# Moving zero fills to SyncE and all loads and result stores to ScalarE in a one-token decode block (forward and backward)

## The chip, the cores and the metric

The kernel runs on one core of a Trainium2 chip. A core has five engines with instruction streams of their own: TensorE (PE in the profile), VectorE (DVE), ScalarE (ACT), GpSimd (POOL) and SyncE (SP). Data move between the device's memory (HBM) and the core's memory (SBUF) by DMA; a DMA is issued by an instruction in the stream of SyncE, ScalarE or GpSimd and is carried by 16 DMA engines. The metric is device time of one execution in microseconds, the median of the runs.

## The reference

One token passes through an attention block with a sliding window over a key/value cache and then a gated bilinear block; the kernel returns the output and the gradients with respect to every input but `B_x`.

```python
D = 448; Hq, Hkv, Sk, Dh = 16, 8, 32768, 256; F = 1792; W = 4096
h  = x + attention(layernorm(x), k_cache[:, :, -W:], v_cache[:, :, -W:], wq, wo)
xn = layernorm(h)
h2 = h + ((xn @ w_gate) * (xn @ w_up)) @ w_down
out, vjp = jax.vjp(f, x, k_cache, v_cache, wq, wo, w_gate, w_up, w_down)
return (out, *vjp(grad_out))
```

All tensors are bf16. The caches have 32768 positions in each of 8 groups and only the last 4096 are used, so the gradients of both caches (`out_2` for K, `out_3` for V, 134 MB each) are zero in 28672 of 32768 rows. Those zeros must be written: 8 groups x 2 tensors x 7 blocks of 2 MB, 235 MB in all. The remaining traffic is about 104 MB: K and V of the window (16 loads of 2 MB), four V loads again for the backward part, the weights (wq twice), 16 stores of 2 MB for the nonzero parts of `out_2` and `out_3`, and the gradients of the weights.

## The kernel before, in words

The kernel is written against a tile framework: it names tiles and operations, and the framework decides the order of instructions in each engine's stream and puts in the semaphores. Each engine executes its stream in order; a DMA instruction that must wait on a semaphore holds everything behind it in that stream. Nearly all of SBUF is one tile, `arena`, cut up by hand with `ar(offset, n)`.

Two names choose the issuing engines (L37, L38): `LD` issues the loads and the stores of results, `ZQ` the zero fills.

1. *Start (L87 to L213).* `zeros`, a region of 8192 columns in each of 128 partitions, is cleared half by VectorE (L87) and half by GpSimd (L88). `LD` loads x, grad_out and wq (L90 to L96). The loop at L114 to L120 issues 103 zero fills of 2 MB on `ZQ`, all reading from `zeros`. `load_kv` (L187) and L194 load K and V of the first groups and `w_down` (`wd_sb`). `layernorm` (L152) uses ScalarE for the square root (L157) and VectorE for its reciprocal (L158) and the rest; L206 and L210 compute q. At L218 VectorE makes 14 products of `w_down` with grad_out, each with a sum, into `d_hh`; they are used only in the middle stage.
2. *Attention (L258 to L324), over 8 groups.* `scores(g + 1)` is called before `moments(g)`. `dots` (L235) transposes K by TensorE (L243), ScalarE copies the transposed blocks back (L260), and row products (L246) make the scores; VectorE copies them (L248) and a softmax follows (L262 to L287). `moments` scales K by the probabilities on VectorE (L298) and multiplies by V on TensorE (L302, L306); ScalarE copies the result (L309). K has three slots and V four (`HELD`); the next load into a slot (L319, L321) waits until TensorE and VectorE have read it.
3. *Middle (L326 to L458).* `wo`, `w_gate` and `w_up` are loaded at L323 to L328 and the layernorm, gated block and its backward are computed, with long runs of VectorE products (L387, L412). `out_0` is stored at L444, and L453 to L458 form the gradient of q.
4. *Backward over 8 groups (L528 to L608).* Each group's V is transposed and multiplied (`dots`), then 16 pairs of TensorE products (L574) fill PSUM tiles `d_ps`, which VectorE (L581, L582) and ScalarE (L578, L579) copy in turn to two of three buffers `stage`. Two stores of 2 MB (L584) send them out. The buffers go round: a later group can't overwrite one until its store has landed. Between groups, the jobs in `plan` (L523) form weight gradients on VectorE (L467, L497) in two buffers `wst` and store them at L478 (`out_5`), L483 (`out_8`), L490 and L505 (`out_6`, `out_7`), L510 and L520 (`out_4`).
5. *Late fills (L610 to L613).* Five fills, 4 of 4 MB and 1 of 2 MB, read `zeros` and the V slot behind it, which L589 clears in the seventh group. They are issued on `LD`, in among the last stores.

The framework guards each DMA with one of a set of completion semaphores that it gives out in turn; a DMA can be issued only when the previous DMA on its semaphore has landed. In the kernel before, GpSimd's fills have one set of eight and SyncE's DMAs another set of eight.

Of the kernel before, what the change touches and what calls it, by code (L numbers as in the profile page):

```python
# [25 lines left out]
ZW = 8192  # L26
# [6 lines left out]
def kernel(  # L33
        ctx, tc, A_x, A_k_cache, A_v_cache, A_wq, A_wo, B_x, B_w_gate, B_w_up, B_w_down, grad_out,
           out_0, out_1, out_2, out_3, out_4, out_5, out_6, out_7, out_8):
    nc = tc.nc
    LD = nc.sync  # L37
    ZQ = nc.gpsimd  # L38

    const = ctx.enter_context(tc.tile_pool(name="const", bufs=1))  # L40
    small = ctx.enter_context(tc.tile_pool(name="small", bufs=2))
# [5 lines left out]
    VB = 16 * KB  # L47
# [5 lines left out]
    def ar(off, n):  # L53
        return arena[:, off:off + n]
# [34 lines left out]
    x_bf = const.tile([1, D], bf16)  # L89
    LD.dma_start(out=x_bf[:], in_=A_x.rearrange("a b d -> (a b) d"))  # L90
    dh2_bc = const.tile([128, D], bf16)
    LD.dma_start(out=dh2_bc[:], in_=grad_out.rearrange("a b d -> (a b) d").to_broadcast([128, D]))
    wq_A = A_wq[0:384, :].rearrange("(p c) j -> p c j", c=3)
    wq_B = A_wq[384:D, :].rearrange("r (h j) -> (r h) j", h=2)
    LD.dma_start(out=wqA, in_=wq_A)
    LD.dma_start(out=wqB, in_=wq_B)  # L96

# [11 lines left out]
    def zero_rows(o, g, n0, n1, f):  # L109
        reg = o[0, g, 0:Sk - W, :].rearrange("s d -> (s d)")[n0 * 128 * ZW:n1 * 128 * ZW]  # L110
        return reg.rearrange("(n p f) -> n p f", p=128, f=f)

    late_jobs = [(out_2, G - 1, 5, 7, 2 * ZW), (out_3, G - 1, 0, 6, 2 * ZW), (out_3, G - 1, 6, 7, ZW)]
    for g in range(G):  # L114
        for o in (out_2, out_3):
            if g == G - 1 and o is out_3:
                continue
            reg = zero_rows(o, g, 0, 5 if g == G - 1 else NZ, ZW)
            for i in range(reg.shape[0]):
                ZQ.dma_start(out=reg[i], in_=zeros)  # L120

# [65 lines left out]
    def load_kv(dst, cache, g):  # L187
        LD.dma_start(out=dst, in_=cache[0, g, Sk - W:, :].rearrange("(p t) d -> p t d", t=T))

# [3 lines left out]
    load_kv(V_slot[1], A_v_cache, 1)  # L193
    LD.dma_start(out=wd_sb, in_=B_w_down.rearrange("(h p b) n -> p h b n", h=2, b=NB))  # L194
    load_kv(K_slot[2], A_k_cache, 2)
# [250 lines left out]
    with tc.tile_pool(name="work2", bufs=2) as work2, tc.tile_pool(name="lnw", bufs=1) as lnw, \  # L446
# [163 lines left out]
        for o, g, n0, n1, f in late_jobs:  # L610
            reg = zero_rows(o, g, n0, n1, f)
            for i in range(reg.shape[0]):
                LD.dma_start(out=reg[i], in_=ar(VB + ZW - f, f))  # L613

# [1 line left out]
_INS = ['A_x', 'A_k_cache', 'A_v_cache', 'A_wq', 'A_wo', 'B_x', 'B_w_gate', 'B_w_up', 'B_w_down', 'grad_out']  # L616
# [26 lines left out]
```

## Time and profile before

| what | value |
|---|---|
| median of three runs | 817.24 us (814.16, 817.24, 819.33) |
| profiled execution's span | 819.2 us |
| busy: TensorE, VectorE, ScalarE, GpSimd | 452.5, 366.3, 192.6, 60.0 us |
| DMA moved | 339.01 MB, mean 414 GB/s over the span |
| GpSimd's queue (q0): packets, MB, share of 16 DMA engines | 14832, 216.01, 62.3% |
| SyncE's queue (q1) | 9494, 122.48, 35.4% |
| GpSimd's 103 fills: issue to landing, median | 59.9 us |
| SyncE's 2 MB stores, issue to landing, median | 27.5 us |
| HBM read, written | 57.89 MB, 280.59 MB |

The profile is one execution. Its span runs from the first to the last instruction. Idle time of an engine is put down to what ended it. "SPq", "DVEq" and the like name the part of an engine that issues and waits; a DMA's landing is the moment when its completion semaphore is full. In the page's slices each digit is the busy share of a fortieth of the span in tenths, 9 meaning 90% or more.

### The profile page before, as it was taken

The page shows a single profiled execution, that of the slowest core. Times are in us where ns is not written, and L with a number is a line of the kernel's source. Part 1 is how long each engine was busy: PE and PEld are TensorE (multiplying, and loading weights), DVE is VectorE, ACT ScalarE, POOL GpSimd, SP SyncE. Part 2 cuts the span into 40 slices and gives each one's busy share as a digit, 9 for nine tenths or more (in the row PEclk, how much of TensorE's full clock was granted, in tenths as well). Part 3 has the DMA queues.
Part 4 walks back from the last instruction along what each step waited for, and adds up shares of the span by engine and source line. Part 5 has one row for each costly group of instructions (what it writes and reads, how often), then busy time and mean ns, then how long its engine had stood idle before and what let it go on. Part 6 is the DMA issues. An engine that isn't in the chain of part 4 may idle for free.

```text
span 819.2 us, 8365 instructions
## 1 busy us (share of the span) xinstructions
PE 452.5 (55%) x3151; PEld 242.9 (30%) x3151; DVE 366.3 (45%) x1153; ACT 192.6 (24%) x301; POOL 60.0 (7%) x112
## 2 busy tenths in 40 slices
PE   0566999999999997510937817352430437111000
PEld 0332545545545554210833413220210213000000
DVE  3023762562652652489234927354455447334000
ACT  0232134134043110200112606141230235123000
POOL 4000000000001100111110000000000000000000
PEclk9967999999999997565876967755655577555555
DMA  8999999999999999999999999999999999999991
GB/s 332 429 427 434 430 426 431 429 429 426 431 428 426 431 413 423 430 429 430 420 425 422 412 428 419 414 426 417 429 413 428 430 430 427 427 424 436 422 413 59
DMA packets 24366, 339.01 MB, mean 414 GB/s; under 512 B 2691, under 2 KB 3334, under 8 KB 4358
## 3 DMA queue, kind: packets, MB, share of 16 engines
q0 software_dynamic: 14832, 216.01, 62.3%
q1 hardware_dynamic: 9494, 122.48, 35.4%
q8 instruction: 24, 0.39, 0.2%
q14 instruction: 16, 0.13, 0.0%
HBM read 57.89 MB, written 280.59 MB: 413 GB/s over the span
## 4 chain that ended last, share of the span: by engine, by line
DMA 28%; DVE 10%; PE 8%; ACT 2%; issue 1%; another core or an unknown queue 1%; SPq 0%; DVEq 0%; ACTq 0%
DMA out_dram<-arena 28%; DVE arena L412 2%; PE rows_ps L246 2%; PE d_ps L574 2%; DVE arena L581 2%; DVE arena L582 2%; PE tr_ps L243 1%; PE dqb_ps L453 1%; DVE arena L467 1%; ACT arena L579 1%; ACT arena L534 1%; DVE arena L387 0%; DVE arena L566 0%; DVE arena L536 0%
## 5 line engine op out<-in xcount | busy, mean ns | idle before, releaser
L298 DVE TENSOR_SCALAR arena<-arena,p_f 128x256 bf16<-128x256 bf16 x512 | 109.3, 280 | 63.0 <-PE M_ps L302 63.0
L574 PE MATMUL d_ps<-arena,rT 32*128 32x512 bf16 x256 | 41.5, 520 | 163.5 <-ACT arena L579 117.3
L302 PE MATMUL M_ps<-arena 128*128 128x512 bf16 x512 | 124.3, 384 | 0.0
L243 PE MATMUL tr_ps<-ident_bf,arena 128*128 128x128 bf16 x1024 | 88.2, 237 | 34.7 <-DVE arena L536 14.4
L120 POOL DMA_DIRECT2D out_dram<-arena x103 | 55.4, 539 | 665.0 <-DMA out_dram<-arena 665.0
L246 PE MATMUL rows_ps<-arena,vpad 128*16 128x512 bf16 x256 | 86.7, 438 | 24.8 <-DVE arena L536 16.4
L243 PEld LDWEIGHTS <-arena 128*128 128x128 bf16 x1024 | 66.3, 106 | 71.3 <-issue 58.9
L260 ACT COPY arena<-tr_ps 128x1024 bf16<-128x1024 bf16 x64 | 61.7, 1015 | 99.0 <-PE tr_ps L243 99.0
L582 DVE CAST arena<-d_ps 128x512 bf16<-128x512 f32 x64 | 43.6, 681 | 84.7 <-DMA out_dram<-arena 84.7
L574 PEld LDWEIGHTS <-rT 32*128 32x128 bf16 x256 | 10.5, 96 | 186.1 <-issue 145.9
L579 ACT CAST arena<-d_ps 128x512 bf16<-128x512 f32 x64 | 38.0, 594 | 108.6 <-DMA out_dram<-arena 108.6
L302 PEld LDWEIGHTS <-arena 128*128 128x128 bf16 x512 | 46.4, 99 | 51.3 <-issue 7.4
L306 PE MATMUL ok_ps<-arena 128*16 128x256 bf16 x512 | 58.7, 274 | 0.9 <-DVE arena L287 0.9
L578 ACT CAST arena<-d_ps 128x512 bf16<-128x512 f32 x64 | 37.6, 588 | 69.9 <-PE d_ps L574 69.8
L581 DVE CAST arena<-d_ps 128x512 bf16<-128x512 f32 x64 | 43.9, 686 | 21.4 <-PE d_ps L574 21.0
L306 PEld LDWEIGHTS <-arena 128*16 128x16 bf16 x512 | 45.2, 90 | 15.6 <-issue 5.1
L534 ACT COPY arena<-tr_ps 128x1024 bf16<-128x1024 bf16 x32 | 32.5, 1015 | 54.3 <-PE tr_ps L243 49.7
L246 PEld LDWEIGHTS <-vpad 128*16 128x16 bf16 x256 | 19.6, 91 | 72.8 <-issue 63.9
L309 ACT COPY arena<-M_ps 128x512 f32<-128x512 f32 x16 | 8.6, 589 | 80.0 <-PE M_ps L302 80.0
L536 DVE COPY arena<-tr_ps 128x1024 bf16<-128x1024 bf16 x32 | 21.8, 683 | 3.6 <-PE tr_ps L243 3.6
L467 DVE TENSOR_SCALAR arena<-arena,xT 128x1792 bf16<-128x1792 bf16 (+1 forms) x9 | 8.0, 893 | 33.1 <-DMA out_dram<-arena 21.5
L412 DVE CUSTOM_DVE_ANT_0 arena<-arena,dh_bc 128x448 bf16<-128x448 bf16 x32 | 20.0, 624 | 1.1
(184 smaller groups left out, 339.0 us busy)
## 6 DMA issues: line engine op xcount, KB each, us to landing
out_dram<-arena POOLq DMA_DIRECT2D x103, 2048.0 KB, 59.9
out_dram<-arena SPq DMA_DIRECT2D x17, 2048.0 KB, 27.5
arena<-in_A_v_cache_dram SPq DMA_DIRECT2D x12, 2048.0 KB, 39.2
arena<-in_A_k_cache_dram SPq DMA_DIRECT2D x8, 2048.0 KB, 21.3
out_dram<-arena SPq DMA_DIRECT2D x4, 4096.0 KB, 42.5
arena<-in_A_wq_dram SPq DMA_DIRECT2D x2, 3072.0 KB
arena<-in_A_wo_dram SPq DMA_DIRECT2D x1, 3584.0 KB
out_dram<-arena SPq DMA_DIRECT2D x3, 1024.0 KB, 44.1
```

Source lines behind the costliest of these rows:

```text
L120: ZQ.dma_start(out=reg[i], in_=zeros)
L243: nc.tensor.transpose(tr_ps[:, dh, i, :], X_sb[:, 4 * q + i, dh * 128:(dh + 1) * 128], ident_bf[:])
L246: nc.tensor.matmul(rows_ps[:], lhsT=pad[:, dh, 16 * q:16 * q + 16], rhs=XT[:, dh].rearrange("p t k -> p (t k)"), start=(q == 0 and dh == 0 ...
L260: sT_ps = dots(K_slot[g % 3], KT_slot, vpad[g % 2], rows1, ps_c, "cols", lambda q, XT, ps: nc.scalar.copy(out=XT, in_=ps))
L298: nc.vector.tensor_scalar(out=pK[:, i, hh, :], in0=K_sb[:, t, :], scalar1=p_f[:, 8 * i + c, hh:hh + 1], scalar2=None, op0=ALU.mult)
L302: nc.tensor.matmul(M_ps[:, vh, :], lhsT=V_sb[:, t, vh * 128:(vh + 1) * 128], rhs=pK[:, i, :, :].rearrange("p h d -> p (h d)"), start=(t == ...
L306: nc.tensor.matmul(ok_ps[:, k, :], lhsT=ppad[g % 2][:, 8 * (t % 4) + t // 4, :], rhs=X_sb[:, t, :], start=(g == 0 and k == 0 and t == 0), ...
L534: nc.scalar.copy(out=XT, in_=ps)
L574: nc.tensor.matmul(d_ps[:, qi].rearrange("p w d -> p (w d)"), lhsT=rT[32 * q:32 * (q + 1), :], rhs=RB_[32 * q:32 * (q + 1), l, :], start=T ...
L579: nc.scalar.copy(out=stK[:, t:t + 2, :], in_=d_ps[:, :, 1, :])
L581: nc.vector.tensor_copy(out=stV[:, t:t + 2, :], in_=d_ps[:, :, 0, :])
L582: nc.vector.tensor_copy(out=stK[:, t:t + 2, :], in_=d_ps[:, :, 1, :])
```

## The change

SyncE issues all zero fills, the 103 early ones and the five late ones, and nothing else. ScalarE issues all loads and all stores of results, 63 DMAs, in the one stream with its copies and activations. GpSimd issues no DMA. No transfer, size, buffer or computation is changed. What the framework then makes of it: SyncE's 108 and ScalarE's 63 DMAs share one set of eight completion semaphores, given out in one common order; and the order of instructions on the other engines shifts, among other places at the start, where VectorE's 14 products at L218 now stand ahead of the reciprocal at L158.

```diff
@@ -34,8 +34,8 @@
     nc = tc.nc
-    LD = nc.sync
-    ZQ = nc.gpsimd
+    LD = nc.scalar
+    ZQ = nc.sync
 
@@ -610,7 +610,7 @@
         for o, g, n0, n1, f in late_jobs:
             reg = zero_rows(o, g, n0, n1, f)
             for i in range(reg.shape[0]):
-                LD.dma_start(out=reg[i], in_=ar(VB + ZW - f, f))
+                ZQ.dma_start(out=reg[i], in_=ar(VB + ZW - f, f))
```

## The prediction

> **What bounds the kernel now.** I read the page's slices and queues first, then stretches of the span by window, then the waits of GpSimd and SyncE, then the timelines at the places that the change touches.
>
> ```profile
> DMA  8999999999999999999999999999999999999991
> GB/s 332 429 427 434 430 426 431 429 429 426 431 428 426 431 413 423 430 429 430 420 425 422 412 428 419 414 426 417 429 413 428 430 430 427 427 424 436 422 413 59
> q0 software_dynamic: 14832, 216.01, 62.3%
> q1 hardware_dynamic: 9494, 122.48, 35.4%
> ```
>
> The DMA engines are full in every slice but the first and the last, at about 427 GB/s. GpSimd's zero fills (q0) are 216 MB, all the rest (q1) 122.5 MB. Nothing runs faster while 339 MB must pass; the engines are off the bound. What matters is whether the DMA engines ever run dry.
>
> ```profile
> 420.00:790.00 370.00, 133.12 (x932) 61.19 (x931) 167.96 (x345) 102.19 (x166) 18.66 (x35) 0.62 1.01 424
> 789.00:814.20 25.20, 0.00 (x0) 0.00 (x0) 0.00 (x0) 0.00 (x0) 0.00 (x0) 0.50 0.45 192
> ...
> POOL out_dram L120 <- DMA out_dram<-arena: 665.0, 95, 12.4
> SPq L638 <- DMA out_dram<-arena: 51.0, 1, 51.0
> ```
>
> The first two lines are stretches (length, busy of five engines, clock, DMA share, GB/s). From 420 to 790 us the rate is 424 GB/s. In the last 25 us the share is 0.45: some of the 16 engines end much before others, which wastes 25.2 x 0.55 = 13.9 us. GpSimd waits 665 us at L120: it always has eight fills under way and issues the next when one lands, so fills are never missing. SyncE's last wait ends near 814 us; some 5 us of span follow.
>
> ```profile
> 75.26 0.63 DVE L218 CUSTOM_DVE_ANT_0 arena<-arena,dh_bc 128x448 bf16<-128x448 bf16 x1 [9.02 <-DMA arena<-in_B_w_down_dram]
> ...
> 22.39 0.19 PE L206 MATMUL qT_ps<-X_b,arena 128*128 128x2 bf16 x1 [12.29 <-DMA arena<-in_A_wq_dram]
> 32.25 1.89 PE L243 MATMUL tr_ps<-ident_bf,arena 128*128 128x128 bf16 x16 [6.71 <-DMA arena<-in_A_k_cache_dram]
> 51.68 0.93 PE L243 MATMUL tr_ps<-ident_bf,arena 128*128 128x128 bf16 x7 [5.43 <-DMA arena<-in_A_k_cache_dram]
> 99.30 0.90 PE L243 MATMUL tr_ps<-ident_bf,arena 128*128 128x128 bf16 x13
> ...
> 45.10 0.68 DVE L248 COPY arena<-rows_ps 16x512 f32<-16x512 f32 x1 [18.95 <-PE rows_ps L246]
> 57.47 3.22 DVE L298 TENSOR_SCALAR arena<-arena,p_f 128x256 bf16<-128x256 bf16 x16
> ...
> 402.74 0.34 SPq L490 DMA_DIRECT2D out_dram<-arena  x1
> ```
>
> These (start, length) date the start: q from 22.4 us, scores of group 0 from 32.3, w_down at 75.3, group 0's moments done at 99.3. ScalarE's copies at L260 then repeat every 31.3 us (100.01, 131.34, 162.66), TensorE being 99% busy. The first large result is stored at 402.7.
>
> **The change, part by part.**
>
> *Issue cost.* An issue on SyncE's queue lasts 0.34 to 0.74 us (L490 above is 0.34). ScalarE takes over 63 of them, 63 x 0.5 = about 32 us in all; it is busy 24% and the DMA engines hide it. GpSimd loses 103 issues of 0.54 us, which held nobody up. The sum has 0 for both. Uncovered, an issue between copies at L578/L579 costs 0.5 us, at most 32.
>
> *Fills tied to the rest.* This is the main term. Before, GpSimd's fills had eight completion semaphores of their own. In the changed program's order all 171 DMAs of SyncE and ScalarE take turns on one set of eight, and each waits until the previous user of its semaphore has landed. At most eight are in flight, and a fill can stand behind a load or store that ScalarE has not been able to issue. The first place where this bites: the 64th fill waits for the store of out_6 at L490 to land. Ahead of it stand 63 fills and all loads, 178 MB. At the rates above the DMA engines are through with them at about 420 us (1 us either way). If L490 issues by then nothing is lost; each us later is lost whole.
>
> *When L490 issues.* The order also moves VectorE's 14 products with w_down (L218) ahead of the first layernorm's reciprocal (L158). The bytes ahead of w_down in its own queue are the same, and the opposite queue is full of fills as before, so it lands again at about 75.3 us; but now everything waits for it. The chain: 75.3 + 14 x 0.67 for L218 (0.67 is the spacing of such products at L412) = 84.7; + 1.4 from reciprocal to X_b (as in the second layernorm, 321.22 to 322.66); + 3.1 for q (22.39 to 25.5); + 0.5; + 10.7 for group 0's scores (32.25 to 45.10, less 2.1 for two transposed blocks that now go ahead of q); + 6.1 softmax (45.10 to 57.47, less 6.3 spent on K of group 1); + 26 for the moments of group 0 with the scores of group 1 (57.47 to 99.30 is 41.8, less 9.0 of waiting for w_down and less 9.4 of its products, is 23.4; TensorE's own work gives 26, which I take). Sum 132.5 against 99.3: 33 us late. ScalarE's own waits are no part of it: its twelfth load, the last before the square root (L157), waits for the fifth fill, which at half rate (9.8 us a fill) lands near 54. In the attention its loads wait for fills that landed earlier, so the period stays 31.3. From 99.3 to 402.7 nothing is shortened that I count on, except 1 us: L490 issues at 435 (418 if only half of the delay survives, 443 if the loads in the middle stage come later).
>
> *After L490.* 339 - 178 = 161 MB are left, at 424 GB/s 380 us: 435 + 380 = 815. Around it the fills are released only as out_6, out_7 and out_5 (L505, L490, L478) land, and a landing takes some 2 us beyond its bytes (x_bf: issued at 0.74, used at 3.23). Two or three such gaps: + 5. Then the stages of the last eight groups: each group's copies wait for the previous group's store (19.9 us at 724.9 in the chain) and then need about 14 us. Between the pairs of stores at L584 the new order puts four to seven fills; with the pair and the jobs that is 29 to 59 us of transfer, more than the 12 + 14 us that a store and the copies behind it need. So transfer stays the bound there, and ScalarE waiting for a semaphore holds up only copies that are early: 0, at most + 15.
>
> *The end.* The late fills (L613) no longer stand behind the stores: SyncE has five transfers, 18.9 MB, to go with the last stores, so there is no bare tail. Of the 13.9 us of uneven ends I keep 3, because the dry spell at 420 us lets all 16 engines start level again (bounds 0 and 14). In the trace's packet records a 16 KB packet takes 618.7 ns in GpSimd's queue and 612.3 in SyncE's; for the 6,300 packets of fills left after L490 that is 6,300 x 6.4 / 16 = 2.5 us less (bounds 0 and 3).
>
> *The sum:* 435 + 380 + 5 + 3 - 2.5 + 5 (after the last landing) = 825 us, against the profiled execution's 819.2. That execution is 0.24% above the median of the three runs, 817.24, so the forecast for a median is 823.
>
> *A rule of the skill.* Before the change, V of group 1 and w_down (3.70 MB) took 51.68 to 75.26, 157 GB/s, where V of group 0 and K of group 1 (4.19 MB) took 32.25 to 51.68, 216 GB/s: w_down's small packets get less than half. The Trainium skill, page "DMA: Bandwidth & Descriptors", section "Queues, rings and completion order", says that each engine serves its queues in turn, packet by packet, and gives SP and ACT a row each. The trace agrees for GpSimd against SyncE; no run here yet shows SyncE against ScalarE.
>
> **The rivals.**
>
> *Nothing changes.* The fills and the rest are the same transfers on the same engines, and both ends of every wait exist before. 819 less the packets' 2.5, so 815 for a median. For it: DMA is full in 38 slices. Against it: one set of semaphores instead of two. The same skill page, section "Issuing engines are not separate DMA queues", holds that the issuing engine matters only for issue time; by that rule this is the case.
>
> *No dry spell, and even engines (faster).* If group 0 is less than 17 us late, L490 issues by 420 and the fills never run out. Then 339 MB at 427 is 794, plus 5 for the slow first slice and 5 at the end: 804, + 2 for a landing gap, 806. It is decided by whether VectorE's wait for w_down is shorter than 75 us. For it: SyncE's packets are quicker and uneven ends may be GpSimd's queue alone. Against it: VectorE's order and the landing at 75.26. The skill's page, section "Latency and other measured facts", suspects GpSimd's descriptor rings of slowing two engines.
>
> *Uneven engines stay and ScalarE's waits hit the copies.* 825 + 11 (all 14 kept) + 15 in the eight groups = 851; half of it 838.
>
> *One line for both queues.* If fills and loads were served strictly in the order of issue, a store would wait behind up to seven fills, 34 us, not 12; 34 + 14 is 48 against 29 to 47 us of transfer: some 15 us in each of five groups, 825 + 75 = 900. Against it: nothing in this trace pairs SyncE with ScalarE.
>
> **How the numbers follow.** Forecast 0.40 (its own range 813 to 834), nothing changes 0.15, faster 0.16, uneven and waiting 0.22, one line 0.07. About 1% (809 to 825) is what a measurement of this kernel can tell. Faster: the third case and a little of the first, 0.18; same: the second and half of the first, 0.37; slower: the rest, 0.45. The range 805 to 850 leaves out the last case and the ends.
>
> **What would show it.** Right: VectorE's L218 before L158 with a wait until 75 us; moments of group 0 done near 132; a slice or two near 420 to 440 us with DMA well under 9; L490 near 435; no long waits of SyncE at L120 elsewhere; a last slice that ends sharply. Wrong: DMA at 9 throughout (no dry spell), group 0 before 116, or DMA slices of 7 and 8 all through the last eight groups.

## The result and the profile after

The changed kernel takes 823.99 us (median of 17 runs, 821.78 to 827.09) against 817.24 us (17 runs, 813.97 to 825.69): ratio 1.0061, 95% interval 1.0035 to 1.0086. It is slower by 0.6%, under the 1% that was named as measurable in advance but outside zero. Ratios here use the runs that were not in a slow state and need not equal the quotient of two medians. The profiled execution after is 824.0 us, before 819.2 us: 4.8 us to explain.

The page of the changed kernel, slices and queues (q1 is SyncE, q10 ScalarE; GpSimd's q0 is gone):

```profile
DMA  8999999999999999999945999999999999999997
GB/s 329 432 430 434 428 428 429 429 428 430 429 429 425 429 427 427 413 428 429 431 190 236 405 414 428 434 425 401 424 433 426 429 426 432 430 430 431 433 436 328
q1 hardware_dynamic: 15552, 234.89, 67.1%
q10 hardware_dynamic: 8774, 103.60, 30.0%
```

Two things differ from before: a dry spell in slices 21 and 22 (4 and 5 tenths), and a last slice of 7 where there was a 1. Stretches of the changed kernel (length, busy of the five engines, clock, DMA share, GB/s):

```profile
420.00:430.00 10.00, 3.41 (x10) 1.93 (x11) 7.13 (x31) 0.00 (x0) 0.00 (x0) 0.50 0.12 52
430.00:440.00 10.00, 10.00 (x50) 8.88 (x49) 2.30 (x4) 1.19 (x2) 0.00 (x0) 0.79 0.01 2
440.00:450.00 10.00, 9.58 (x61) 8.07 (x60) 6.13 (x11) 2.71 (x5) 0.00 (x0) 1.00 0.83 347
460.00:790.00 330.00, 164.36 (x912) 68.74 (x911) 166.36 (x332) 100.79 (x166) 0.00 (x0) 0.59 1.01 425
818.00:824.00 6.00, 0.00 (x0) 0.00 (x0) 0.00 (x0) 0.00 (x0) 0.00 (x0) 0.50 0.25 107
```

From 420 to 450 the missing share is 8.8 + 9.9 + 1.7 = 20.4 us. From 460 to 790 nothing is missing. The kernel before ended otherwise; its stretch from the point where the share falls to its last landing:

```profile
795.00:814.00 19.00, 0.00 (x0) 0.00 (x0) 0.00 (x0) 0.00 (x0) 0.00 (x0) 0.50 0.29 122
```

That is 19 x 0.71 = 13.5 us missing, and 5 us with no transfer follow. So 20 us are lost in the middle and some 14 us come back at the end. Two timelines of the changed kernel, VectorE's and ScalarE's, show why the dry spell ends when it does:

```profile
75.80 0.63 DVE L218 CUSTOM_DVE_ANT_0 arena<-arena,dh_bc 128x448 bf16<-128x448 bf16 x1 [67.34 <-DMA arena<-in_B_w_down_dram]
...
85.02 0.15 DVE L158 RECIPROCAL mv<-mv 1x1 f32<-1x1 f32 x1
101.10 0.68 DVE L248 COPY arena<-rows_ps 16x512 f32<-16x512 f32 x1 [10.60 <-PE rows_ps L246]
```

```profile
56.17 1.28 ACT L157 ACT_TABLE_LOAD   x1 [56.17 <-DMA out_dram<-arena]
...
129.05 1.07 ACT L309 COPY arena<-M_ps 128x512 f32<-128x512 f32 x2 [9.13 <-PE M_ps L302]
...
136.02 0.34 ACTq L188 DMA_DIRECT2D arena<-in_A_k_cache_dram  x1
...
439.77 0.37 ACTq L490 DMA_DIRECT2D out_dram<-arena  x1
```

VectorE waits 67 us for w_down, and the first reciprocal comes after its products. Group 0's moments are copied out at 129.05 (before: 97.45), L490 issues at 439.8 (before: 402.7), and the DMA engines run again from 440. SyncE's waits at L120 confirm who is waiting (us in total, times, longest), and its timeline shows the 64th fill:

```profile
SPq L120 <- DMA out_dram<-arena: 402.1, 51, 35.6
...
444.45 0.81 SPq L120 DMA_DIRECT2D out_dram<-arena  x2
```

The longest, 35.6 us, is the one for out_6: the 63rd fill is issued at 408.5 and the 64th, which has out_6's semaphore, at 444.45, when out_6 has landed. SyncE also waits up to 30.5 us at L120 for a V load and 29.7 us for `wo`, where the prediction expected no other long wait; the DMA engines stay full in those waits. The median fill takes 31.3 us from issue to landing, against 59.9 before: fills wait in SyncE, not in the DMA engines.

### The profile page after: what moved, and what is told of

Its sections match the earlier page's. It is cut to its first block, busy times and chain, and to the rows that moved or that the text cites. A ratio compares the mean times of both kernels' runs of the same rounds, so it can differ in the third digit from the quotient of the medians.

```text
span 824.0 us, 8353 instructions
## 1 busy us (share of the span) xinstructions
PE 481.8 (58%) x3151; PEld 250.4 (30%) x3151; DVE 374.2 (45%) x1153; ACT 190.6 (23%) x301; POOL 4.6 (1%) x9
## 5 line engine op out<-in xcount | busy, mean ns | idle before, releaser
L298 DVE TENSOR_SCALAR arena<-arena,p_f 128x256 bf16<-128x256 bf16 x512 | 110.0, 283 | 59.5 <-PE M_ps L302 59.5
L574 PE MATMUL d_ps<-arena,rT 32*128 32x512 bf16 x256 | 58.1, 545 | 120.0 <-DVE arena L582 82.5
L243 PE MATMUL tr_ps<-ident_bf,arena 128*128 128x128 bf16 x1024 | 99.5, 251 | 41.0 <-DMA arena<-in_A_k_cache_dram 25.0
L302 PE MATMUL M_ps<-arena 128*128 128x512 bf16 x512 | 121.5, 380 | 0.0
L243 PEld LDWEIGHTS <-arena 128*128 128x128 bf16 x1024 | 73.1, 112 | 96.8 <-issue 70.5
L246 PE MATMUL rows_ps<-arena,vpad 128*16 128x512 bf16 x256 | 96.2, 470 | 7.6 <-DVE arena L536 3.0
L260 ACT COPY arena<-tr_ps 128x1024 bf16<-128x1024 bf16 x64 | 61.6, 1014 | 135.9 <-PE tr_ps L243 135.9
L302 PEld LDWEIGHTS <-arena 128*128 128x128 bf16 x512 | 46.0, 98 | 51.9 <-issue 6.3
L574 PEld LDWEIGHTS <-rT 32*128 32x128 bf16 x256 | 12.6, 97 | 157.0 <-issue 91.2
L581 DVE CAST arena<-d_ps 128x512 bf16<-128x512 f32 x64 | 44.1, 688 | 34.8 <-PE d_ps L574 34.7
L306 PE MATMUL ok_ps<-arena 128*16 128x256 bf16 x512 | 58.2, 273 | 0.9 <-DVE arena L287 0.9
L306 PEld LDWEIGHTS <-arena 128*16 128x16 bf16 x512 | 45.1, 90 | 13.8 <-issue 3.4
L218 DVE CUSTOM_DVE_ANT_0 arena<-arena,dh_bc 128x448 bf16<-128x448 bf16 x14 | 8.7, 624 | 67.8 <-DMA arena<-in_B_w_down_dram 67.3
L536 DVE COPY arena<-tr_ps 128x1024 bf16<-128x1024 bf16 x32 | 22.0, 687 | 13.5 <-PE tr_ps L243 12.5
L458 ACT ACTIVATE arena<-dqb_ps 128x512 bf16<-128x512 f32 x8 | 4.8, 597 | 68.1 <-PE dqb_ps L456 59.7
L412 DVE CUSTOM_DVE_ANT_0 arena<-arena,dh_bc 128x448 bf16<-128x448 bf16 x32 | 20.0, 624 | 1.1
## 6 DMA issues: line engine op xcount, KB each, us to landing
out_dram<-arena SPq DMA_DIRECT2D x104, 2048.0 KB, 31.3
out_dram<-arena ACTq DMA_DIRECT2D x16, 2048.0 KB, 21.8
out_dram<-arena ACTq DMA_DIRECT2D x3, 1024.0 KB, 13.3
```

What stands on the lines that cost most here:

```text
L243: nc.tensor.transpose(tr_ps[:, dh, i, :], X_sb[:, 4 * q + i, dh * 128:(dh + 1) * 128], ident_bf[:])
L246: nc.tensor.matmul(rows_ps[:], lhsT=pad[:, dh, 16 * q:16 * q + 16], rhs=XT[:, dh].rearrange("p t k -> p (t k)"), start=(q == 0 and dh == 0 ...
L260: sT_ps = dots(K_slot[g % 3], KT_slot, vpad[g % 2], rows1, ps_c, "cols", lambda q, XT, ps: nc.scalar.copy(out=XT, in_=ps))
L298: nc.vector.tensor_scalar(out=pK[:, i, hh, :], in0=K_sb[:, t, :], scalar1=p_f[:, 8 * i + c, hh:hh + 1], scalar2=None, op0=ALU.mult)
L302: nc.tensor.matmul(M_ps[:, vh, :], lhsT=V_sb[:, t, vh * 128:(vh + 1) * 128], rhs=pK[:, i, :, :].rearrange("p h d -> p (h d)"), start=(t == ...
L306: nc.tensor.matmul(ok_ps[:, k, :], lhsT=ppad[g % 2][:, 8 * (t % 4) + t // 4, :], rhs=X_sb[:, t, :], start=(g == 0 and k == 0 and t == 0), ...
```

## The experiments

Questions: is it the late attention, through the shared semaphores, that costs the time? And why are the ends even now? The rivals: ScalarE's issuing, the queue that carries the fills, or the dry spell as a thing that levels the engines.

**e1: the first layernorm ahead of the loads** (the changed kernel otherwise).

```
+    rstd1, xnT_f, X1_b = layernorm(x_bf[:], bf16, "ln1")
     load_kv(K_slot[0], A_k_cache, 0)
     ...
-    rstd1, xnT_f, X1_b = layernorm(x_bf[:], bf16, "ln1")
```

> The changed kernel with the first layernorm written ahead of the loads of K, V and w_down, so that its square root on ScalarE and its reciprocal on VectorE no longer stand behind the wait for w_down; the fills stay tied to the loads and stores. Theory (the dry spell at 420 to 440 us costs the time, because L490 comes late, and the even ends belong to the fills being on SyncE's queue): group 0 is done near 120 us instead of 136, L490 issues at 420 to 426 instead of 440, the dry spell shrinks from 20 us to 0 to 6, and the time is 805 to 812. Rival 1 (the even ends are only a gift of the dry spell): L490 moves as above but the last 25 us are uneven again, some 10 us come back, time 815 to 820. Rival 2 (the dry spell is not what sets the time): 822 to 826, as the changed kernel.

Measured: 812.64 us, ratio to the kernel before 0.9913 (0.9878 to 0.9948). The moments of group 0 are copied at 114.5, L490 issues at 425.6. Its stretches:

```profile
420.00:430.00 10.00, 9.58 (x58) 8.06 (x58) 3.64 (x6) 3.29 (x5) 0.00 (x0) 1.00 0.45 188
430.00:440.00 10.00, 10.00 (x66) 9.23 (x66) 6.00 (x14) 1.79 (x3) 0.00 (x0) 1.00 0.75 310
...
790.00:805.00 15.00, 0.00 (x0) 0.00 (x0) 0.00 (x0) 0.00 (x0) 0.00 (x0) 0.50 0.99 424
805.00:811.20 6.20, 0.00 (x0) 0.00 (x0) 0.00 (x0) 0.00 (x0) 0.00 (x0) 0.50 0.16 69
```

The dry spell falls from 20 to 8 us, the ends stay even, and the span falls by 12.8 us. The dry spell and the time end just above the theory's 0 to 6 us and 805 to 812. One moved line turns the split into a gain of 0.9%: the loss against the kernel before came from the order that the change brought about. The tie still costs the 8 us that are left.

**e5: the products with w_down done twice.**

```
-    for h in range(2):
+    for h in [0, 1] * 2:
```

> The changed kernel with the 14 products with w_down done twice (the second time gives the same numbers), all ahead of the first layernorm's reciprocal on VectorE. It adds 14 x 0.67 = 9.4 us of VectorE work at about 85 us and no transfer. Theory (each us by which L490 is late past 420 us is lost whole): group 0 near 145, L490 near 449, dry spell 29 us, time 833 (829 to 836). Rival (the delay is taken up by slack, since DMA is the bound and VectorE is idle most of the span): 822 to 826.

Measured: 834.83 us, ratio 1.018 (1.0134 to 1.0225); the span is 833.4, 9.4 more than the changed kernel's. L490 is at 448.6, 8.8 later.

```profile
420.00:430.00 10.00, 0.00 (x0) 0.00 (x0) 9.48 (x31) 0.00 (x0) 0.00 (x0) 0.50 0.69 293
430.00:440.00 10.00, 4.56 (x13) 2.83 (x14) 6.05 (x27) 0.00 (x0) 0.00 (x0) 0.50 0.00 0
440.00:450.00 10.00, 10.00 (x54) 9.04 (x54) 2.30 (x4) 1.79 (x3) 0.00 (x0) 0.85 0.09 35
```

VectorE is idle for more than half of the span, and yet 9.4 us of work on it near 85 us cost 9.4 us at the end. Of these, 8.8 are in the dry spell (29.3 us missing against 20.5); the other 0.6 is less than two executions of one kernel differ by.

**e6: the same in the kernel before.**

> The kernel before with the 14 products with w_down done twice: the control of e5. It delays VectorE by 9.4 us near 85 us, but the fills have semaphores of their own and nothing waits for L490. Theory: L490 near 412, no dry spell, time within 2 us of the kernel before (815 to 820). Rival (lateness of the attention costs in any split): 824 to 829, with the loss at the end of the run.

Measured: 819.61 us, ratio 0.9994 (0.9953 to 1.0035). No cost, as expected, but it proves less than was meant: here the products stand between the multiplications of the moments and fill waits there, and L490 issued at 403.7, not 412. The delay never reached the stores, so this says nothing on lateness without the tie; e3 does.

**e3: late attention without the tie** (fills on GpSimd, all else on ScalarE).

```
     LD = nc.scalar
-    ZQ = nc.sync
+    ZQ = nc.gpsimd
     ...
-                ZQ.dma_start(out=reg[i], in_=ar(VB + ZW - f, f))
+                LD.dma_start(out=reg[i], in_=ar(VB + ZW - f, f))
```

> Fills on GpSimd as in the kernel before, loads and stores on ScalarE as in the changed one, late fills (L613) on ScalarE too. GpSimd's fills have semaphores of their own; VectorE's order is the changed kernel's. Theory (tie makes the dry spell; GpSimd's queue makes the uneven ends): no dry spell at 420 to 440 us, L490 after 430, uneven ends of 10 to 14 us as before, and up to 15 us more because the last stage starts 33 us later and ScalarE issues the late fills between its copies: 815 to 830. Rival (moving loads and stores to ScalarE costs time by itself, its waits holding up copies): above 830, with DMA slices of 7 or 8 in the last third. Rival (the unevenness was the pairing of GpSimd with SyncE): 804 to 812.

Measured: 823.32 us, ratio 1.0031 (1.0004 to 1.0058). L490 is as late as in the changed kernel, 437.8, and there is no dry spell at 420 to 440. But:

```profile
420.00:440.00 20.00, 15.33 (x70) 12.56 (x71) 7.61 (x29) 1.79 (x3) 2.54 (x5) 0.70 1.00 424
754.00:764.00 10.00, 1.22 (x6) 0.31 (x6) 2.46 (x4) 1.11 (x3) 0.00 (x0) 0.50 0.24 102
...
800.00:808.00 8.00, 4.76 (x18) 0.92 (x16) 5.16 (x8) 5.21 (x10) 0.00 (x0) 0.50 0.00 0
```

The fills were not held back at 420, and from 754 nothing is left of GpSimd's queue; the last pair of stores (L584, at 809.3; before 758.9) finds the DMA engines idle ahead of it. So time is lost without the tie too, as the upper part of the theory's range had it, but at the end of the run. That the late attention alone costs it is not shown. From L490 to the last pair of stores the kernel before takes 356 us and e3 372, and e3's late fills (L613) stand among ScalarE's copies:

```profile
760.09 0.58 ACT L579 CAST arena<-d_ps 128x512 bf16<-128x512 f32 x1 [18.27 <-DMA out_dram<-arena]
...
763.49 0.34 ACTq L613 DMA_DIRECT2D out_dram<-arena  x1
```

ScalarE waits 18 us for a store to land, and the next late fill is issued only behind that wait, while the DMA engines have a share of 0.24. So the rival has a part in it: its slices of 7 and 8 are there (7, 8, 8 and 4 at the end of the page's DMA row), though the time stays below its 830. How much is lateness and how much ScalarE's order of issue, no run separates.

**e4: fills on SyncE, loads and stores on GpSimd.**

```
-    LD = nc.scalar
+    LD = nc.gpsimd
     ZQ = nc.sync
```

> The fills on SyncE as in the changed kernel, but loads and stores on GpSimd, so that the fills have completion semaphores of their own and wait only for other fills. VectorE's order keeps the products with w_down ahead of the reciprocal, so group 0 and L490 stay late. Theory (the tie through the eight shared semaphores makes the dry spell, not the late attention by itself): no slice under 8 between 400 and 460 us although L490 issues after 430. Time then by the ends: with even ends (unevenness belongs to the queue that carries the fills, GpSimd's) 804 to 812; with uneven ends (unevenness comes with any run without a dry spell, or with any use of GpSimd's queue) 814 to 822. Rival (the late attention itself leaves nothing to transfer near 420 us): the dry spell stays and the time is 820 to 826.

Measured: 816.21 us, ratio 0.9968 (0.9938 to 0.9999). It misses as a test of lateness: with ScalarE free of loads the square root and the reciprocal (14.7 us) come early again and L490 is at 413.7. It is of use for the ends. Fills on SyncE's queue end unevenly too:

```profile
795.00:811.00 16.00, 0.00 (x0) 0.00 (x0) 0.00 (x0) 0.00 (x0) 0.00 (x0) 0.50 0.46 196
```

**e7 and e8: the products moved off the path.** In both, the 14 products move from L216 into the loop over the groups and wait for the softmax of group 2; e7 is e1 with this, e8 the kernel before with this.

```
+            if g == 1:
+                nc.vector.tensor_scalar(out=one_late[:], in0=p_next[:, 0, 0:1], scalar1=0.0, scalar2=1.0, op0=ALU.mult, op1=ALU.add)
+                nc.vector.tensor_scalar(out=dh2_bc[:], in0=dh2_bc[:], scalar1=one_late[:], scalar2=None, op0=ALU.mult)
+                for h in range(2):
+                    for b in range(NB):
...
```

> The changed kernel with the first layernorm ahead of the loads, as in e1, and the 14 products with w_down made to wait for the softmax of group 2 (their second operand is multiplied by a 1.0 that is worked out from it), so that no engine waits for w_down near 75 us. DMAs, queues, semaphores and their order are those of e1. Theory (dry spell = how late L490 is past 420): group 0 done at 82 to 92, L490 at 387 to 400, no slice under 9 between 400 and 460. Then the ends decide what the uneven ends of the kernel before came from. If from GpSimd's queue: the last 20 us are as sharp as in the changed kernel, time 802 to 808. If every run without a dry spell ends unevenly: 812 to 818. Rival (the tie costs by itself, in the last eight groups): DMA slices of 7 or 8 after 500 us and 815 or more.

> The kernel before (fills on GpSimd, loads and stores on SyncE), with the products made to wait for the softmax of group 2 as in e7: the control of e7 for the attention's earlier end alone. Theory (the kernel before is bound by transfers; its fills are never missing, its ends are uneven): L490 near 387 to 395, the rest as before, 815 to 820. Rival (it is the earlier attention, not the split, that gains in e7): 803 to 810.

Measured: e7 811.61 us, ratio 0.991 (0.9878 to 0.9942); e8 818.54 us, ratio 0.9978 (0.9939 to 1.0016). In e8 L490 issues at 396.4, 6 us earlier than in the kernel before, so the earlier attention alone gains nothing that can be told, as the theory had it. e7 fell short: group 0 is done at 102, not 82 to 92, because ScalarE now stands at its twelfth load (timeline of ScalarE in e7, where the copies of L260 are L257):

```profile
62.55 0.34 ACTq L188 DMA_DIRECT2D arena<-in_A_v_cache_dram  x1
62.93 1.93 ACT L257 COPY arena<-tr_ps 128x1024 bf16<-128x1024 bf16 x2 [58.26 <-DMA arena<-in_A_v_cache_dram]
```

L490 issues at 416.2, ahead of 420, and still some time is lost:

```profile
422.00:429.00 7.00, 6.99 (x44) 6.28 (x43) 0.77 (x3) 0.60 (x1) 0.00 (x0) 1.00 0.42 178
...
804.00:809.00 5.00, 0.00 (x0) 0.00 (x0) 0.00 (x0) 0.00 (x0) 0.00 (x0) 0.50 0.17 72
```

The next fill needs out_6 to have landed, not to have been issued. In the trace's records of out_6's semaphore the first of 16 increments comes at 422.6 and the last at 428.13, 12 us after the issue; the next fill is issued at 428.15. So 416 was too late by some 6 us or more, for the share falls from 422 on.

**e9, e10, e11: earlier still.** e9 is e7 with the loads of K and V of group 2, V of group 3 and w_down moved behind the scores of group 0 and so between ScalarE's copies. e10 and e11 also move the loop of the fills behind the loads and hold it back until K of group 0, or V of group 1, has landed.

```
         p_next = scores(0)
+        load_kv(K_slot[2], A_k_cache, 2)
+        load_kv(V_slot[2], A_v_cache, 2)
+        load_kv(V_slot[3], A_v_cache, 3)
+        LD.dma_start(out=wd_sb, in_=B_w_down.rearrange("(h p b) n -> p h b n", h=2, b=NB))
```

```
+    nc.gpsimd.tensor_scalar(out=zeros[:, 0:1], in0=K_slot[0][:, 0, 0:1], scalar1=0.0, scalar2=None, op0=ALU.mult)
+    for g in range(G):
+        for o in (out_2, out_3):
...
```

> e7 with the loads of K and V of group 2, V of group 3 and w_down written after the scores of group 0, so that ScalarE issues them between its copies and not ahead of them. In e7 its first copy waited until 62.9 us behind the twelfth load. Runs so far say: span = 804 + the time for which the DMA engines ran dry near 420 to 440 us (after 20, e1 8, e7 4, e5 29). Theory: copies of group 0 start near 32 us and end near 58, group 0 done at 84 to 92, L490 at 395 to 408, no dry spell at all. If the uneven ends of the kernel before belong to the use of GpSimd's queue: last 20 us sharp, span 803 to 806, median 804 to 809. If it takes a dry spell, however short, to make the 16 engines end together: a tail of 8 to 14 us of low share returns, 812 to 818.

> e9 with the zero fills made to wait until K of group 0 has landed (GpSimd writes one column of the zero tile from K times 0.0), so that the first loads have the DMA engines to themselves. All DMAs stay on SyncE and ScalarE. By the program, 61 fills then stand ahead of the first that waits for a large store (L505, the store after L490), about 174 MB, which are through near 412 us. Theory: K lands near 18 us and not 32, group 0 done at 70 to 82, L490 at 380 to 398, the fills never run out, no slice under 8 from the second to the last but one. If even ends belong to having nothing on GpSimd's queue: last 20 us sharp, span 803 to 806, median 804 to 808. If they come from a dry spell: a tail of 8 to 14 us of low share, span 812 to 818. Rival (a dry spell comes anyway, by another wait): dry spell of x us, span 804 + x.

> e10 with the fills waiting for V of group 1 instead of K of group 0, that is some 15 us later; 58 fills stand ahead of the first that waits for L505, about 168 MB, through near 398 us. Theory: L490 at 372 to 390, again no dry spell and the same two cases for the ends: span 803 to 806, or 812 to 818. It tells whether more lead of the attention is worth anything once no transfer is missing (theory: nothing, within 2 us of e10). If the loads alone do not keep the DMA engines full in the first 40 us, the second slice shows it and the span is longer by that.

Measured: 812.49 us (ratio 0.9898, 0.986 to 0.9937), 811.35 us (0.9922, 0.9895 to 0.9949), 810.87 us (0.9917, 0.9884 to 0.995). L490 came to 414.1, 400.3 and 386.1 (expected: 395 to 408, 380 to 398, 372 to 390), but each reordering also changed which fill stands behind which store, and the fills ran out earlier as well: 7.7, 5.0 and 4.3 us were missing between 340 and 460. No version was without a dry spell, which none of the three expected, so these runs could not settle what makes the ends even. They end within 2 us of e1 and e7; e11, with the lowest median, is 0.8% below the kernel before.

**e12 and e13: a dry spell made on purpose, in kernels without the tie.** e12 is the kernel before, e13 is e4, each with one wait: all fills under way have to land after the 53rd.

```
                 ZQ.dma_start(out=reg[i], in_=zeros)
+                if (o, g, i) == (out_3, 3, 3):
+                    nc.gpsimd.memset(zeros[:, 0:1], 0.0)
```

> The kernel before, with one wait added: after its 53rd fill GpSimd writes a zero into the zero tile, for which all fills under way (at most eight) have to land first, so that the DMA engines run dry once near 385 us, at a time when SyncE has nothing to transfer. Fills stay on GpSimd, nothing is tied to L490. Theory (the 16 engines drift apart as long as no DMA waits for all of them, whatever queue carries the fills; a dry spell lets them start level): a dry tail of some 7 us near 385, and at the end a tail of 4 us in place of the 19 us of the kernel before; span 804 + 6 + 2 + 3 = 815, so 0.3 to 0.8% less than the kernel before in spite of the wait. Rival (uneven ends belong to GpSimd's queue and come at the end in any case): the tail stays over 12 us and the wait is paid on top, span 824 to 828, 0.5 to 1% more.

> e4 (fills on SyncE, loads and stores on GpSimd, two sets of semaphores) with the wait of e12: after the 53rd fill all fills under way have to land once, near 380 us. It tells apart why the last stretch after a dry spell ended with a tail of 12 us in e12 and of 3 to 5 us in the changed kernel, e1, e5, e7, e9, e10 and e11. Theory A (it is the queue that carries the fills): fills are on SyncE here, so the tail after the wait is 3 to 5 us, span 804 + 6 + 2 + 3 = 815. Theory B (it is the shared set of eight semaphores, by which fills, loads and stores wait for each other): the two sets are apart here, so the tail is 10 to 13 us as in e12, span 818 to 824. Both expect a tail of 6 to 8 us at the wait near 380.

Measured: e12 823.13 us, ratio 1.0041 (1.0006 to 1.0076); e13 819.22 us, ratio 1.0008 (0.9975 to 1.004). Stretches at the wait and at the end, e12 first, then e13:

```profile
371.00:380.00 9.00, 0.00 (x0) 0.00 (x0) 8.51 (x29) 0.00 (x0) 0.41 (x2) 0.50 0.18 78
...
806.00:818.00 12.00, 0.00 (x0) 0.00 (x0) 0.00 (x0) 0.00 (x0) 0.00 (x0) 0.50 0.39 168
```

```profile
371.00:383.00 12.00, 2.09 (x9) 1.81 (x9) 9.19 (x31) 0.00 (x0) 0.10 (x1) 0.50 0.30 128
...
809.00:816.00 7.00, 0.00 (x0) 0.00 (x0) 0.00 (x0) 0.00 (x0) 0.00 (x0) 0.50 0.13 56
```

At 371 both queues show the same tail: the 16 engines are 8 to 10 us apart after 370 us, whichever queue carries the fills. After the dry spell GpSimd's fills end with a tail of 12 us, SyncE's with one of 7. The theory that a dry spell is enough falls: e12 was to be faster than before and is slower, as its rival had it (span 824 to 828; it is 824.6). e13 lies between its two theories: its tail of 7 us is nearer to theory A, the queue of the fills, its span of 817.3 nearer to theory B.

The traces hold a more direct measure. They record 16 increments of a DMA's semaphore, as many as there are DMA engines. I take the time from the first increment to the last as the lag between the first and the last engine. For the fills that land in each stretch and have all their increments on record it is (us; the first two kernels, without a dry spell, are divided at 425 us):

| kernel | fills on | from 340 us to the dry spell | from there to 480 us | largest, 700 to 760 us |
|---|---|---|---|---|
| before | GpSimd | 8.6 to 12.8 | no dry spell; 11.0 to 17.5 | 44.1 |
| e4 | SyncE | 9.3 to 14.2 | no dry spell; 13.6 to 19.4 | 25.9 |
| e12 | GpSimd | 7.5 to 8.0 | 0.4 to 4.0 | 29.8 |
| e13 | SyncE | 9.3 to 13.7 | 0.2 to 3.2 | 14.8 |
| after | SyncE | 7.4 to 13.8 | 0.2 to 1.5 | 8.9 |
| e11 | SyncE | 9.1 to 9.8 | 1.7 to 6.5 | 15.0 |

In all of them the lag is 1 to 5 us around 100 us and grows, also where nothing is issued on GpSimd (after, e11). The dry spell takes it down, to 0.2 to 0.4 us in the first fills of e12, e13 and the changed kernel. So a dry spell does level the engines, on either queue. What differs is how fast they drift apart again: in these profiles faster with fills on GpSimd (e12) than on SyncE. e13 is no worse than e11, which has the shared set.

**All spans by one sum.** For each profile I added length x (1 - DMA share) over stretches of 10 us, a share above 1 counting as 1, with one last stretch from 780 us to the end (e6 is left out: its profiled execution, 829.32 us, lies 10 us above its median):

| kernel | span us | missing 340 to 460 | missing from 780 | missing elsewhere | span less all missing |
|---|---|---|---|---|---|
| before | 819.2 | 0.0 | 18.4 | 4.3 | 796.5 |
| after | 824.0 | 20.5 | 4.8 | 3.7 | 795.0 |
| e1 | 811.2 | 8.6 | 5.6 | 3.7 | 793.3 |
| e5 | 833.4 | 29.3 | 5.9 | 3.4 | 794.8 |
| e3 | 821.7 | 0.1 | 13.3 | 11.4 | 796.9 |
| e4 | 812.6 | 0.0 | 10.4 | 6.1 | 796.1 |
| e7 | 809.0 | 4.1 | 4.1 | 3.7 | 797.1 |
| e8 | 816.5 | 0.0 | 16.8 | 3.2 | 796.5 |
| e9 | 810.6 | 7.7 | 5.2 | 4.1 | 793.6 |
| e10 | 809.5 | 5.0 | 7.1 | 3.0 | 794.4 |
| e11 | 809.3 | 4.3 | 7.0 | 3.7 | 794.3 |
| e12 | 824.6 | 8.0 | 13.8 | 4.9 | 797.9 |
| e13 | 817.3 | 8.4 | 7.5 | 5.8 | 795.6 |

The last column stays within 5 us while the spans differ by 24: the time of every version is its transfers plus the time in which DMA engines had nothing to do.

## Why the prediction came out right, point by point

*The bound.* Right. The table above is the statement that nothing runs faster while 339 MB must pass.

*The tie and the dry spell (the main term).* Right in mechanism and size: the fills ran out at 420, as worked out, and came back with L490. That each us past 420 is lost whole is shown by e5 (L490 8.8 us later, 8.8 us more missing) and nearly so by e1 (L490 14.2 us earlier, 11.9 us less missing). Wrong is the point from which it decides: nothing was to be lost with L490 at 420. e7 has it at 416.2 and loses 4 us; out_6 has to land, on the slowest of 16 engines, which took 12 us there. The forecast of 806 for that rival was too low for this reason; e7's span is 809.0. And e3 (ratio 1.0031) shows that without the tie time can be lost at the end of the run instead; whether lateness alone does that stays open.

*When L490 issues.* At 439.8; predicted was 435. The chain holds for VectorE: w_down lands at 75.8 (75.3), products done at 85.0 (84.7), moments of group 0 31.6 us late (33). Up to group 0's first L298, 106.45 against 106.5 from the terms, it is right to 0.1 us. The missing 5 us are mostly in the next term, 26 us for the moments of group 0 with the scores of group 1, which measured 29.5 (to 135.92, the first transposition after them). TensorE's 64 products for `ok_ps` (L306) come in there. Before, 47 of them were done by 89.5 us, while VectorE was held by w_down's products, and 17 were left behind the last L302; now 63 are left, which takes 7.05 us in place of 2.02 (the first line is from the kernel before):

```profile
97.34 2.02 PE L306 MATMUL ok_ps<-arena 128*16 128x256 bf16 x17
...
128.94 7.05 PE L306 MATMUL ok_ps<-arena 128*16 128x256 bf16 x63
```

So ScalarE's next copies (L260) start at 136.63, 7.6 us after L309, where it was 2.6 us before. ScalarE's load at L188, issued at 136.02, stands between, but the copy waits for TensorE's transposition. The other 1.4 us are the 1 us counted as shortened, which was not, and 0.4 us up to the last group. The wait for the fifth fill before L157 ended at 56.2 (54 predicted), hidden behind w_down as said; e7, with w_down out of the way, shows what it costs uncovered: copies from 62.9 instead of 32.

*After L490.* From 439.8 to 824.0 there are 384.2 us, of which 1.7 are missing from 440 to 450 and 6 x 0.75 = 4.5 from 818 on; the 161 MB took the other 378, against 380 less the packets' 2.5. The landing gaps were set at 5 and cost 1.7. The last eight groups cost nothing, as forecast: share 1.01 from 460 to 790. ScalarE's 63 issues cost nothing beyond the waits named.

*The end.* Set at 3 us of uneven ends and 5 after the last landing, it came to 4.5 in all. That the dry spell levels the engines is right: the lag falls from 8.0 to 0.2 us. That this alone makes even ends is not: they drift apart again. e12 shows that a dry spell leaves 13.8 us missing where GpSimd carries the fills, against 18.4 without it; e13 and e4 have 7.5 and 10.4 where SyncE does; the kernels with everything on one set of semaphores have 4.1 to 7.1. Each is one profile, so the steps between them are rough: GpSimd's fills end less evenly, but e13's 7.5 can't be told from e10's 7.1, so an effect of the shared set itself is not shown. Why engines drift at all was not settled: the trace does not say which engine carried a packet, and no kernel with the shared set ran without a dry spell.

*Packets.* In the packet records the 16 KB packets of fills take 616.2 ns in SyncE's queue here and 618.6 ns in e4, not the 612.3 ns of SyncE's loads and stores before: it goes with the fills, not with the queue. By these rows the term is 6,300 x 2.5 / 16 = 1.0 us, not 2.5.

*The sum.* The forecast's terms make 825.5, written as 825. With what was measured it is 439.8 + 378 + 1.7 + 4.5 = 824.0, the span; it must come out, for the 378 is what the others leave. The forecast's parts were off by +4.8 (L490), +0.5 (transfers), -3.3 (gaps) and -3.5 (the end), which nearly cancel. That the total is closer than its parts is luck. The step of 2 us from the span to the median (825 to 823) was not there either: they are 824.0 and 823.99.

*The Trainium skill's rules.* By the Trainium skill, page "DMA: Bandwidth & Descriptors", section "Issuing engines are not separate DMA queues", nothing was to change but issue time. For the transfers the trace agrees (1.01 share, 425 GB/s from 460 to 790). The 20 us come from the order in which issuers wait (444.45 for the 64th fill). The same page of the Trainium skill, section "Queues, rings and completion order", has SP and ACT served in turn: w_down on ScalarE's queue against SyncE's fills landed at 75.80, on SyncE's against GpSimd's at 75.26, so the case that was open agrees. The rival with one line for both is out: ScalarE's 2 MB stores land a median 21.8 us after their issue, and the time is not near 900. The Trainium skill's section "Latency and other measured facts" there suspects GpSimd's rings of slowing two engines: the smaller tails with SyncE's fills fit in direction, but the changed kernel issues nothing on GpSimd, and its engines are 8 us apart ahead of the dry spell all the same.

## What to carry to other kernels

In a kernel bound by transfers, list for each issuing engine what its next DMA waits for, in program order: moving issues to another engine can tie transfers together that were independent, and it moves the engine's other work too. Here a wait for one load on VectorE at 75 us set the time at which a store at 440 us let the fills go on, and moving one line was worth about 1.5% of the time (ratio 0.9913 against 1.0061). Add up length x (1 - DMA share) over the span before arguing about causes: it says at once how much there is to find, and where, though not why.

## What was not expected of the hardware

The 16 DMA engines do not end together: after 370 us of full use, when no fill was issued any more, the last one finished 8 to 10 us after the share began to fall (e12, e13), and at the end of the kernel before 19 us after. A wait for the fills ends only behind that tail (in e12 at 379.2, where the share began to fall at 371), so a single wait took 9 x 0.82 = 7 us of DMA time, with nothing else to wait for. The lag shows in every kernel, with fills on GpSimd or on SyncE, and grows while fills follow each other without a break: from 2 us at 100 us to 44 in the kernel before.
